# One order for all engines: operand sums in the attention stage, z additions and sums between the hops, weight loads earlier on SP's queue

## The chip, the cores and the metric

The kernel runs on one core of one Trainium2 chip. The metric is the device time of one execution in microseconds; lower is better. Times are medians of several runs.

## The reference

The input is `x` of 2048 rows by 512. The output adds to it a linear attention over 32 heads of 16, and a gated feed-forward block with F = 1792:

```python
phi = lambda t: jnp.where(t > 0, t + 1, jnp.exp(t)) + 1e-6
pq, pk = phi(q), phi(k)                      # q, k, v from layernorm(x) @ wqkv
kv = jnp.einsum("bhsd,bhse->bhde", pk, v)
z = jnp.einsum("bhsd->bhd", pk)
num = jnp.einsum("bhqd,bhde->bhqe", pq, kv)
den = jnp.einsum("bhqd,bhd->bhq", pq, z)[..., None] + 1e-6
A = reshape(num / den) @ wo
B = (silu(xn @ w_gate) * (xn @ w_up)) @ w_down   # xn = layernorm(x)
return x + A + B
```

## The kernel before, in words

**A recording layer and five engines.** The kernel records its operations with `K.add(engine, function, r=..., w=...)`. Each engine runs its own operations in the order in which they were recorded, and the layer puts a semaphore wait wherever an operation reads or overwrites what another engine or a DMA has written. The order is therefore written by hand, as text: a string in `run(...)` (L769 to L780) for the attention stage, and the string `STAGE` (L34 to L58) for the feed-forward (FFN) stage. A word is a letter for the step and a number for the tile. A Python loop (L925 to L942) records the tail. PE is TensorE, DVE VectorE, ACT ScalarE, POOL GpSimd, and SP the queue that issues most DMAs.

**Attention stage.** The rows fall into 16 tiles of 128. For each tile t DVE takes statistics (`S`: `bn_stats` L382 and `bn_aggr` L385), ACT makes 1/std (`R`), and DVE or POOL writes the normalized row (`L` L450, `P` L465). SP turns it with a DMA transpose into `xnT` (`D`, `dmat` L534). PE projects the turned row to K and Q (`K` and `Q`, `proj` L547, four bf16 matmuls of 128x512 each, called a group below). Then phi: ACT takes an exponential from the PSUM bank (L565), POOL clips it (L574) and DVE adds the bank's own value (`phi_sum`, L581; `s` for K, `u` for Q). PE accumulates x' * phi(K) into banks 0 to 3 (`G`, `gacc` L592, another group of four). Tiles 0, 1 and 2 are turned on PE instead, and K of tile 1 and Q of tile 0 use banks 1 and 0, so that `gacc(0)` overwrites banks that the phi sums of rows 0 and 2 read. The sum over rows of phi(K), `z`, is added up by `z_add` (L604): one half on DVE (`zv`), one on POOL (`zp`).

**FFN stage.** hT = silu(gate) * up is made for 512 rows by 128 columns at a time. Four pieces of the 56 are made plainly (`u_mm` L643, `u_sil` L654, `u_hop` L661: the "hop" is DVE's multiplication from a PSUM bank into hT). The rest are made in quads of 2x2 pieces by seven products in place of eight: `product(k, ...)` (L708). Products 1 and 2 are bf16 pairs of matmuls (L711), 3 to 7 fp32r pairs (L717), whose operands are sums and differences of the blocks. `x_form(p, k)` (L690) makes the row sums S from `xnT`, on DVE for k = 0 to 3, each 128x1024 (L700), and on ACT for k = 4. `w_form(i, k)` (L673) makes the weight differences T on POOL (L688). A product written into a bank is combined there: ACT copies banks (`fork` L722, `keep7` L726), DVE adds (`add_c` L730, `add_d` L735), ACT takes silu (`q_sil`), DVE or POOL multiplies (`q_hop` L749). A bank's next product waits for these. PE also runs kv (L789), spread among the matmuls of a plain piece; DVE masks it (`kv_mask` L792, which writes `kvT`).

**Tail.** `pz_mul` (POOL), `divide` and `scale_turn` (DVE, then an SP transpose) make num/den per tile; `o_h` (L859) and `o_a` (L866) are the output matmuls, and `oout` adds x and stores.

**Weight loads.** `BIG` (L757) lists them: T0 and T1 the first halves of gate and up (896 KB each), T2 the V part of wqkv and T3 wo (512 KB each), T4 and T5 the second halves (896 KB each). All go out on SP's queue, the same that issues the transposes of `xn` and the loads of the rows of x.

Of the kernel before, what the change touches and what calls it, by code (L numbers as in the profile page):

```python
# [159 lines left out]
def bass_parallel_sum__linear_attn_block__swiglu_ffn__prompt_kernel(nc, A_x, A_wqkv, A_wo, B_x, B_w_gate, B_w_up, B_w_down, out):  # L160
# [5 lines left out]
    with contextlib.ExitStack() as es:  # L166
# [594 lines left out]
        steps.update({"U": pair, "T": lambda t: BIG[t](), "H": lambda k: x_form(0, k), "V": lambda k: w_form(1, k)})  # L761

        def run(text):
            words = [(w[0], int(w[1:].split(":")[0]), [int(c) for c in w.split(":")[1]] if ":" in w else None)
                     for w in text.split()]
            for k, t, cs in words:
                steps[k](t) if cs is None else steps[k](t, cs)

        run("""  # L769
            c2 c0 M2 S0 S2 O0 d0 M1 e0 S1 h0 d2 Q0:0 e2 h2 F1 C1 Q0:1 Q2:01 l4 W1 S3 R0 l13 Q0:3 r0 l6 R3 l10  # L770
            Q0:2 Q2:2 j2 j1 K0:1 y0 l11 L3 K0:2 Q2:3 y2 J0 n0 K2:12 n2 l7 K0:3 K0:0 w1 S4 K2:0 K2:3 K1:013 X3 x0
            l8 S13 u0 x2 m0 Y3 s0 R13 m2 K1:2 Q1 P13 K3:02 l9 u2 x1 m1 K3:13 s2 S9 R4 l5 Q3 T1 y1 s1 R9 l14 L9
            D13 x3 P4 D4 n1 G0 S10 G2 m3 y3 D9 n3 G1 K13 u1 s3 u3 x13 l15 S5 P1 m13 s13 Q13 K4 y13 R10 K9 R5 n13
            G3 Q4 S14 x4 x9 P5 S7 m4 s4 G13 R7 y4 P10 u13 m9 l12 R14 n4 D5 S8 G4 D10 T0 Q9 s9 P2 S6 K5 x5 u4 S15
            P14 L7 m5 y9 D14 G9 n9 Q10 Q5 R6 s5 u9 y10 S12 D7 R8 G5 K10 y5 n10 u10 L8 P6 K14 n5 x10 m10 x14 D6
            u5 Q14 y14 D8 R15 s10 K7 S11 G10 L15 R12 x7 m14 s14 Q7 n14 R11 T2 u14 D15 y7 K6 m7 G14 s7 D1 Q8 P0
            L11 D11 n7 L12 x6 u7 K8 y8 x8 m6 n8 K15 m8 s6 D0 D12 x15 u8 K11 x11 s8 m15 Q6 m11 T3 y6 n6 s15 Q15
            Q11 s11 y15 K12 y11 u6 x12 G7 m12 G6 n11 Q12 y12 G8 s12 D2 n12 n15 V1 V3 G12 H0 u12 U0 H2 G11 G15 u15
            u11 H4 V2 V4 V0 U14 H1 H3 T4 T5
        """)  # L780

        def gt_evac(c, eng):
# [197 lines left out]
```

## Time and profile before

| | us |
|---|---|
| median of 3 runs | 216.93 |
| lowest, highest | 216.58, 217.29 |
| the profiled execution, its own time | 216.53 |
| its span in the profile | 215.2 |

The span runs from the first to the last instruction of the profile, the time covers what lies around it as well. The page gives PE as busy for 203.7 us of the span, DVE 165.2, POOL 122.3 and ACT 94.4. Rows of the page's groups hold the line, the engine, the operation, out<-in, the form and the count, then busy time and mean ns of one, then idle time of the engine ahead of it and what ended it. A timeline row holds start, duration, engine, line, operation and form, and in brackets the engine's idle time ahead of it, with the releaser. The granted clock is the share of the full TensorE clock that the throttle let through.

### The profile page before, as it was taken

How to read it: one execution, taken by the hardware profiler on the slowest of the kernel's cores; microseconds unless marked ns; L12 is line 12 of the kernel's file. 1: busy time of each engine (PE TensorE's matmuls, PEld its weight loads, DVE VectorE, ACT ScalarE, POOL GpSimd, SP SyncE). 2: the span in 40 equal slices, each digit the busy share in tenths (PEclk: the TensorE clock that was granted, in tenths of full speed). 3: DMA queues.
4: the chain of work that ended last, by engine and by line, in shares of the span. 5: the costliest groups of instructions: out<-in, count | busy, mean ns of one | idle time of the engine just before them, and what ended most of it. 6: DMA issues, size and time to landing. Idle time of an engine off the chain costs nothing.

```text
span 215.2 us, 2788 instructions
## 1 busy us (share of the span) xinstructions
PE 203.7 (95%) x943; PEld 112.7 (52%) x960; DVE 165.2 (77%) x269; ACT 94.4 (44%) x192; POOL 122.3 (57%) x140
## 2 busy tenths in 40 slices
PE   8999999996648999999999999999999999999996
PEld 4444434442223576676676676675544444444446
DVE  3899998647899987677777779999379999975112
ACT  5986456642813576866676676675100000000000
POOL 3498866569999197976986938401175345310000
PEclk9999999999996999999999999999999999999999
DMA  5963596591000000000000120762188223224101
GB/s 160 360 222 92 163 157 171 129 326 59 0 0 0 0 0 3 0 0 0 0 3 0 27 49 0 260 108 47 41 249 223 68 81 97 70 81 73 49 24 50
DMA packets 31038, 18.53 MB, mean 86 GB/s; under 512 B 18864, under 2 KB 30896, under 8 KB 31024
## 3 DMA queue, kind: packets, MB, share of 16 engines
q1 hardware_dynamic: 27856, 15.48, 27.2%
q10 hardware_dynamic: 3168, 2.88, 4.5%
q8 instruction: 7, 0.11, 0.2%
q14 instruction: 7, 0.06, 0.1%
HBM read 12.06 MB, written 2.10 MB: 66 GB/s over the span
## 4 chain that ended last, share of the span: by engine, by line
PE 88%; DVE 8%; DMA 2%; issue 1%; ACT 0%
PE pb L717 28%; PE pb L861 22%; PE pb L557 12%; PE pb L711 10%; PE pb L867 6%; DVE S L700 5%; PE pb L596 5%; DMA xnT<-xn 2%; PE pb L649 2%; PE pb L372 2%; DVE hT L665 1%; DVE zacc L611 1%; DVE zacc L613 0%; PE pb L515 0%; PE pb L507 0%
## 5 line engine op out<-in xcount | busy, mean ns | idle before, releaser
L717 PE MATMUL pb<-S,T 128*128 128x512 f32 x260 | 70.7, 415 | 0.3 <-DVE kvT L795 0.3
L717 PEld LDWEIGHTS pb<-S,T 128*128 128x128 f32 x260 | 48.5, 188 | 14.6 <-DVE kvT L795 1.0
L861 PE MATMUL pb<-wd,hT 128*128 128x512 bf16 (+2 forms) x248 | 51.2, 355 | 0.3
L861 PEld LDWEIGHTS pb<-wd,hT 128*128 128x128 bf16 x252 | 23.4, 98 | 25.0 <-issue 0.5
L753 DVE TENSOR_TENSOR hT<-pb,sil 128x512 bf16<-128x512 f32 x39 | 26.6, 682 | 10.9 <-PE pb L717 10.4
L822 POOL TENSOR_TENSOR pz<-pq,zbc 128x512 f32<-128x512 bf16 x16 | 22.3, 1404 | 18.5 <-DVE den L829 17.4
L753 POOL TENSOR_TENSOR hT<-end,sil 128x512 bf16<-128x512 f32 x13 | 15.1, 1161 | 24.8 <-DVE end L737 22.6
L711 PE MATMUL pb<-xnT,wgu 128*128 128x512 bf16 x98 | 26.6, 389 | 0.3
L724 ACT ACTIVATE pb<-pb 128x512 f32<-128x512 f32 x26 | 15.2, 584 | 25.8 <-PE pb L711 25.8
L747 ACT ACTIVATE sil<-pb 128x512 bf16<-128x512 f32 x39 | 23.1, 596 | 6.6 <-PE pb L717 6.5
L557 PE MATMUL pb<-wqkv,xnT 128*128 128x512 bf16 x103 | 24.0, 379 | 0.6 <-DMA xnT<-xn 0.5
L876 DVE TENSOR_TENSOR out_sb<-pb,x 128x512 bf16<-128x512 f32 (+2 forms) x18 | 11.3, 625 | 14.9 <-PE pb L867 12.4
L737 DVE TENSOR_TENSOR end<-pb,mid 128x512 f32<-128x512 f32 x26 | 17.7, 681 | 5.3 <-PE pb L717 5.3
L688 POOL TENSOR_TENSOR T<-wgu 128x512 fp32r<-128x512 bf16 x14 | 18.5, 1328 | 4.6 <-PE pb L717 4.3
L577 POOL TENSOR_SCALAR ef<-ef 128x512 bf16<-128x512 bf16 x26 | 15.8, 617 | 9.2 <-ACT ef L572 9.2
L572 ACT ACTIVATE ef<-pb 128x512 bf16<-128x512 f32 x26 | 15.1, 593 | 12.3 <-PE pb L557 12.3
L732 DVE TENSOR_TENSOR pb<-pb,mid 128x512 f32<-128x512 f32 x26 | 18.0, 692 | 2.0 <-PE pb L717 2.0
L844 DVE TENSOR_TENSOR pq<-pq,rden 128x512 bf16<-128x512 bf16 x16 | 18.0, 1126 | 0.4
L688 POOL TENSOR_TENSOR T<-wgu,T 128x512 fp32r<-128x512 bf16 x14 | 17.8, 1276 | 0.1
L557 PEld LDWEIGHTS pb<-wqkv,xnT 128*128 128x128 bf16 x104 | 10.1, 98 | 13.1 <-DMA xnT<-xn 1.0
L728 ACT ACTIVATE mid<-pb 128x512 f32<-128x512 f32 x26 | 15.6, 600 | 1.0 <-DVE end L737 0.5
L711 PEld LDWEIGHTS pb<-xnT,wgu 128*128 128x128 bf16 x104 | 8.6, 100 | 13.6 <-issue 7.1
(90 smaller groups left out, 234.0 us busy)
## 6 DMA issues: line engine op xcount, KB each, us to landing
x<-in_A_x_dram ACTq DMA_DIRECT2D x16, 128.0 KB, 2.6
out_dram<-out_sb SPq DMA_DIRECT2D x15, 128.0 KB, 1.9
x_sb<-in_A_x_dram SPq DMA_DIRECT2D x14, 128.0 KB, 4.2
wgu<-in_B_w_up_dram SPq DMA_DIRECT2D x2, 896.0 KB, 7.8
wgu<-in_B_w_gate_dram SPq DMA_DIRECT2D x2, 896.0 KB, 6.1
wd<-in_B_w_down_dram SPq DMA_DIRECT2D x1, 1792.0 KB, 8.8
wqkv<-in_A_wqkv_dram ACTq DMA_DIRECT2D x4, 128.0 KB, 5.1
wqkv<-in_A_wqkv_dram SPq DMA_DIRECT2D x4, 128.0 KB, 4.9
```

Source lines behind the costliest of these rows:

```text
L557: fns.append(lambda e, c=c, first=first, last=last: e.matmul(banks[b][:, :], src[:, c, :], wqkv[:, c, col:col + D], start=first, stop=last))
L577: K.add("pool", lambda e: e.tensor_scalar(out=buf, in0=buf, scalar1=top, scalar2=0.0, op0=ALU.min, op1=ALU.max), r=[bkey] + tkeys, w=[bkey])
L688: K.add("pool", lambda e: e.tensor_tensor(out=out, in0=a, in1=b, op=ALU.subtract), r=keys + op, w=[("T", ring, k)])
L711: fns = [(lambda e, h=h: e.matmul(banks[a][:, :], wgu[:, m, 2 * (k - 1) + h, 2 * i * P:(2 * i + 1) * P], xnT[:, 2 * p, 2 * (k - 1) + h, :] ...
L717: fns = [(lambda e, h=h: e.matmul(banks[bank][:, :], TT[RING[i]][tk][:, m, h, :], SS[p][sk][:, h, :], start=(k == 7 and h == 0), stop=(h = ...
L732: K.add("dve", lambda e: e.tensor_tensor(out=banks[c][:, :], in0=banks[b][:, :], in1=mid[:, m, :], op=ALU.add), r=[B(b), ("mid", m)], w=[B ...
L737: K.add("dve", lambda e: e.tensor_tensor(out=end[:, m, :], in0=banks[b][:, :], in1=mid[:, m, :], op=ALU.add), r=[B(b), ("mid", m)], w=[("e ...
L747: K.add("act", lambda e: e.activation(sils[r][:, q, :], src, ACT.Silu), r=[key], w=[("sil", 4 * r + q)])
L753: K.add("pool" if q == 3 else "dve", lambda e: e.tensor_tensor(out=hT[:, C, fc, :], in0=src, in1=sils[r][:, q, :], op=ALU.mult), r=[key, ( ...
L822: K.add("pool", lambda e: e.tensor_tensor(out=pz[:, t % 2, :].rearrange("q (g p) -> q g p", g=NG), in0=pq[:, t, :].rearrange("q (g p) -> q ...
L844: K.add("dve", lambda e: e.tensor_tensor(out=heads(pq[:, t, :]), in0=heads(pq[:, t, :]), in1=rden[:, i, :][:, :, None].broadcast_to([P, NH ...
L861: K.add("pe", [(lambda e, fc=fc: e.matmul(banks[bank][:, 0:hi - lo], hT[:, C, fc, jj * P:(jj + 1) * P], wd[:, fc, lo:hi], start=start and ...
```

## The change

One string, `PLAN`, now holds the whole program in place of the two strings and the loop. Words without a slash are steps of the attention stage, words with one go to `go()`. Three functions are cut in two, so that the parts can be recorded apart: `z_sum` (with `z_store` and `z_spread`), `scale_turn` (with `turn_pq`) and `oout` (with `ostore`). Every operation of before is still recorded; none is added. The order changes on every engine. The core of the diff (word lists cut):

```diff
-STAGE = """
-zp8 Ea0 Ev3 Uu1 S4 S2 Ug1 t02 Ea1 1g10 zv0 zp9 7g10 Us1 S0 Ea2 t32 Zg10 Uh1 Ug15 Ag10 zv1 t12 S1 6g10 Us15 kvm
...
+PLAN = """
...
+K0:1 T2 y0 Q2:2 K2:12 L3 j2 Q2:3 R13 n0 K2:0 S9 y2 K2:3 K0:2 K0:3 P13 S10 K0:0 x2
...
+G12 /S01 G11 /S20 G15 Q12 /S10 /Ea0 /Ug14 y12 /Uu14 n12 /Us14 /t01 u12 /Ea1 /Ug0 /t41 /Uh14 /Uu0 /zv1 /Us0 /t32
...
-        def pair(j):
-            u_mm(j, 0)
-            u_sil(j)
-            u_mm(j, 1)
-            u_hop(j)
...
-            c2 c0 M2 S0 S2 O0 d0 M1 e0 S1 h0 d2 Q0:0 e2 h2 F1 C1 Q0:1 Q2:01 l4 W1 S3 R0 l13 Q0:3 r0 l6 R3 l10
...
+        def z_store():
             K.add("sp", lambda e: e.dma_start(zrow[0].rearrange("(p g) -> p g", g=NG), zc[:, :]),
                   r=[("zc",)], w=[("zrow",)], dma=True)
+
+        def z_spread():
...
+        def turn_pq(t):
...
+        def ostore(t, lo, hi):
...
-        for w in STAGE.replace("ZB", "ZB ZT").split():
-            go(w)
...
+        for w in PLAN.split():
+            if w[0] == "/":
+                go(w[1:])
+            else:
+                t_, _, cs_ = w[1:].partition(":")
+                steps[w[0]](int(t_), [int(c) for c in cs_]) if cs_ else steps[w[0]](int(t_))
```

In PLAN `/Spk` is `x_form(p, k)`. The lines of the kernel after are shifted by 24 in the attention helpers (L586 is L610) and by 18 behind them (L700 is L718).

**SP's queue, from the first loads of rows of x on.** In the rows, `x_sb` are row loads, `wgu` and `wqkv` weights, `wo` the output weights, and `xnT<-xn` the transposes. Before:

```order
L315 DMA x_sb<-in_A_x_dram 128x512 x9
L315 DMA wgu<-in_B_w_up_dram 128x4x896
L315 DMA x_sb<-in_A_x_dram 128x512
L535 DMA_TRANSPOSE xnT<-xn 128x4x128 x3
L315 DMA x_sb<-in_A_x_dram 128x512 x2
L535 DMA_TRANSPOSE xnT<-xn 128x4x128 x2
L315 DMA wgu<-in_B_w_gate_dram 128x4x896
L535 DMA_TRANSPOSE xnT<-xn 128x4x128 x4
L315 DMA wqkv<-in_A_wqkv_dram 128x4x512
L535 DMA_TRANSPOSE xnT<-xn 128x4x128 x5
```

And of the change, the same place, behind the nine row loads that stand first here as well:

```order
L339 DMA wgu<-in_B_w_gate_dram 128x4x896
L339 DMA wqkv<-in_A_wqkv_dram 128x4x512
L559 DMA_TRANSPOSE xnT<-xn 128x4x128
L339 DMA x_sb<-in_A_x_dram 128x512 x2
L339 DMA wgu<-in_B_w_up_dram 128x4x896
L559 DMA_TRANSPOSE xnT<-xn 128x4x128 x2
L339 DMA wgu<-in_B_w_gate_dram 128x4x896
L559 DMA_TRANSPOSE xnT<-xn 128x4x128
L339 DMA wgu<-in_B_w_up_dram 128x4x896
L339 DMA wo<-in_A_wo_dram 128x4x512
L339 DMA x_sb<-in_A_x_dram 128x512
```

All six weight loads now stand among the first four transposes (those of tiles 13, 4, 9 and 5); the last three loads stand between tile 5's transpose and those of tiles 0 and 10.

**DVE ahead of the first accumulation.** `BN_STATS` and `BN_AGGR` are one tile's statistics, `SCALAR_TENSOR_TENSOR` are phi sums (`pq` of Q, `pk` of K). Before, up to the phi sum that `gacc(0)` waits for:

```order
L382 BN_STATS stats<-x_sb 128x6
L385 BN_AGGR mv<-stats 128x2
L382 BN_STATS stats<-x_sb 128x6
L385 BN_AGGR mv<-stats 128x2
L586 SCALAR_TENSOR_TENSOR pq<-pb,flo,ef 128x512
L586 SCALAR_TENSOR_TENSOR pk<-pb,flo,ef 128x512
L586 SCALAR_TENSOR_TENSOR pq<-pb,flo,ef 128x512
L586 SCALAR_TENSOR_TENSOR pk<-pb,flo,ef 128x512
```

Of the change, at the same place:

```order
L406 BN_STATS stats<-x_sb 128x6
L409 BN_AGGR mv<-stats 128x2
L475 TENSOR_SCALAR xn<-x_sb,mv,rstd 128x512
L462 TENSOR_SCALAR tmp<-x_sb,mv,r 128x512
L406 BN_STATS stats<-x_sb 128x6
L409 BN_AGGR mv<-stats 128x2
L406 BN_STATS stats<-x_sb 128x6
L409 BN_AGGR mv<-stats 128x2
L610 SCALAR_TENSOR_TENSOR pq<-pb,flo,ef 128x512
L406 BN_STATS stats<-x_sb 128x6
L409 BN_AGGR mv<-stats 128x2
L610 SCALAR_TENSOR_TENSOR pk<-pb,flo,ef 128x512 x2
```

The phi sum of Q of tile 2 follows as the next row. Statistics of two more tiles, and two layernorm rows, now stand ahead of the four phi sums; the tiles are 13, 9, 10 and 4.

**DVE at the end of the attention stage.** `S_57`, `S_58`, `S_59` and `S_62` are `x_form(0, 0)`, `(0, 1)`, `(0, 2)` and `(1, 0)`, and `hT<-pb,usil` is a plain piece's hop. Before:

```order
L586 SCALAR_TENSOR_TENSOR pk<-pb,ef 128x512
L700 TENSOR_TENSOR S_57<-xnT 128x1024
L586 SCALAR_TENSOR_TENSOR pq<-pb,ef 128x512
L665 TENSOR_TENSOR hT<-pb,usil 128x512
L700 TENSOR_TENSOR S_59<-xnT 128x1024
L586 SCALAR_TENSOR_TENSOR pq<-pb,ef 128x512 x2
L665 TENSOR_TENSOR hT<-pb,usil 128x512
L700 TENSOR_TENSOR S_58<-S_57,xnT 128x1024
```

Of the change, the same place:

```order
L610 SCALAR_TENSOR_TENSOR pk<-pb,ef 128x512
L610 SCALAR_TENSOR_TENSOR pq<-pb,ef 128x512
L718 TENSOR_TENSOR S_62<-xnT 128x1024
L718 TENSOR_TENSOR S_59<-xnT 128x1024
L718 TENSOR_TENSOR S_58<-S_57,xnT 128x1024
L610 SCALAR_TENSOR_TENSOR pq<-pb,ef 128x512
L689 TENSOR_TENSOR hT<-pb,usil 128x512
```

`S_57` and the first z addition now stand eight and ten rows above this place, among the phi sums; three more sums stand ahead of the last phi sum, and the first hop follows it with no sum between.

**Elsewhere.** POOL's z additions of tiles 8 to 11 move behind the start of the third quad, its first five weight differences stand earlier among the steps of the attention stage, and in the FFN stage the sums of PE's results stand fewer products ahead of the product that needs their bank. In the tail the matmuls of neighbouring tiles are mixed, with `o_h` of a tile ahead of `o_a` of an earlier one.

More of the change, by code (lines that the diff above doesn't have):

```diff
@@ new lines @@
+G3 P10 x9 S11 x4 Q4 u13 D10 m4 G13 y4 m9 s4 R14 P14 Q9 L7 s9 K5 S6 y9 n4 D14 G4 n9 u4 x5 u9 R15 D1 Q10 m5 P2 s5
+Q5 y10 S8 R6 D2 K10 n10 R11 S12 P6 K14 x10 u10 D7 y5 G9 m10 L11 R8 n5 D6 R12 G5 s10 x14 L12 Q14 L15 m14 u5 G10
+L8 y14 /zv0 D8 K7 n14 s14 Q7 /S00 D15 x7 K6 m7 y7 u14 D11 G14 n7 s7 x6 u7 D12 Q8 m6 /t11 s6 K8 y8 K15 n8 x8 u8
+K11 m8 x15 s8 Q6 m15 x11 s15 Q15 m11 y6 /t31 s11 Q11 n6 K12 y11 u6 G7 n11 x12 u11 y15 G6 m12 n15 s12 G8 /t21 u15
+G12 /S01 G11 /S20 G15 Q12 /S10 /Ea0 /Ug14 y12 /Uu14 n12 /Us14 /t01 u12 /Ea1 /Ug0 /t41 /Uh14 /Uu0 /zv1 /Us0 /t32
@@ L56 @@
+/oo15.256.384 /os15.256.384 /oo15.384.512 /os15.384.512
 """
@@ L760, in bass_parallel_sum__linear_attn_block__swiglu_ffn__prompt_kernel @@
                lambda: dload("sp")]
[L761 to L769, printed above, removed]
-            c2 c0 M2 S0 S2 O0 d0 M1 e0 S1 h0 d2 Q0:0 e2 h2 F1 C1 Q0:1 Q2:01 l4 W1 S3 R0 l13 Q0:3 r0 l6 R3 l10
[L771 to L780, printed above, removed]
+        steps["T"] = lambda t: BIG[t]()
         def gt_evac(c, eng):
```

103 lines of the change are left out of this document (59 added, 44 removed).

## The prediction, made before the kernel was run

> **What bounds the kernel now.** I read the page's slices first, then PE by stage, then the one stage where PE is not full. On the page:
>
> ```profile
> span 215.2 us, 2788 instructions
> ...
> PE   8999999996648999999999999999999999999996
> ...
> PEclk9999999999996999999999999999999999999999
> ```
>
> Slices are 5.4 us. PE is full in all but three of the inner ones, and there alone is its clock lower. Busy time by stretch (columns: stretch, length, PE, PEld, DVE, ACT, POOL, granted clock, DMA share, GB/s):
>
> ```profile
> 40.00:50.00 10.00, 9.95 (x47) 4.58 (x47) 5.55 (x8) 5.95 (x9) 6.14 (x9) 1.00 0.80 256
> 50.00:60.00 10.00, 5.85 (x29) 2.43 (x28) 8.57 (x8) 4.58 (x8) 9.92 (x9) 1.00 0.01 1
> 60.00:66.00 6.00, 2.93 (x23) 1.65 (x22) 6.00 (x6) 0.60 (x1) 6.00 (x4) 0.89 0.00 0
> 66.00:72.00 6.00, 5.72 (x21) 2.66 (x19) 6.00 (x7) 2.49 (x5) 3.63 (x3) 0.83 0.00 0
> 80.00:90.00 10.00, 9.93 (x45) 6.69 (x45) 6.37 (x11) 7.79 (x16) 8.67 (x9) 1.00 0.01 2
> 160.00:170.00 10.00, 9.95 (x48) 4.52 (x47) 9.69 (x16) 0.00 (x0) 4.51 (x4) 1.00 0.69 182
> ```
>
> The FFN stage (80 to 90) and the tail (160 to 170) run PE at 9.93 and 9.95 of 10: nothing can be won there, only lost. What can be won lies between 50 and 70 us, where DVE is full. PE's timeline there, with the wait in brackets:
>
> ```profile
> 48.84 1.89 PE L596 MATMUL pb<-pk,xn 128*128 128x512 bf16 x8
> 52.54 1.90 PE L649 MATMUL pb<-xnT,wgu 128*128 128x512 bf16 x8 [1.81 <-DVE pq L586]
> 55.23 1.90 PE L649 MATMUL pb<-xnT,wgu 128*128 128x512 bf16 x8 [0.79 <-DVE hT L665]
> ...
> 59.58 0.38 PE L649 MATMUL pb<-xnT,wgu 128*128 128x512 bf16 x1 [1.56 <-ACT pb L724]
> 59.80 0.82 PE L789 MATMUL pb<-GT,wqkv 128*128 128x128 bf16 x8
> ...
> 65.03 1.89 PE L649 MATMUL pb<-xnT,wgu 128*128 128x512 bf16 x4 [3.02 <-DVE hT L665]
> 66.71 1.70 PE L711 MATMUL pb<-xnT,wgu 128*128 128x512 bf16 x4
> 68.69 2.28 PE L717 MATMUL pb<-S,T 128*128 128x512 f32 x8 [0.28 <-DVE kvT L795]
> ```
>
> Five waits: 1.81 + 0.79 + 1.56 + 3.02 + 0.28 = 7.46 us. And after the 3.02 the matmuls run slower. The steady pace is in the chain of waits (start, length, engine, tile, line, count):
>
> ```profile
> 95.39 2.31 PE pb L717 x10
> 97.70 0.88 PE pb L711 x4
> ```
>
> An fp32r matmul takes 0.231, four bf16 ones take 0.87, 0.217 each. From 65.03 to 68.41 (68.69 less its wait of 0.28) the 8 bf16 matmuls took 3.38 where 1.73 would do, and the 8 of the next row 2.28 where 1.85 would: 2.08 us of lowered clock (0.89 and 0.83 in the windows). So the hole is worth 7.46 + 2.08 = **9.54 us**. What DVE did in it:
>
> ```profile
> 49.65 2.23 DVE L700 TENSOR_TENSOR S<-xnT 128x1024 fp32r<-128x1024 bf16 x1
> ...
> 60.90 1.38 DVE L611 TENSOR_SCALAR zacc<-pk,rstd 128x512 f32<-128x512 bf16 x1
> 62.20 2.17 DVE L700 TENSOR_TENSOR S<-xnT 128x1024 fp32r<-128x1024 bf16 x1
> 64.30 0.68 DVE L665 TENSOR_TENSOR hT<-pb,usil 128x512 bf16<-128x512 f32 x1
> ```
>
> The 3.02 us wait is for the hop at 64.30, which stood behind a z addition and an operand sum, 3.5 us of work that nobody needed yet. The 1.81 is for a phi sum behind the operand sum of 49.65. A queue in the wrong order, then, more than too much work.
>
> **Part 1, the operand sums go ahead (gain).** The changed DVE order puts one z addition and four sums before the last phi sum, one of them well inside the attention stage, where the PE matmuls leave DVE idle 4.45 of 10 us (window 40 to 50). The hops come right behind, each with at most one addition ahead. POOL's z additions of this stretch move into the FFN stage. If nothing else happened, the five waits and the slow clock would go: 9.54, less about 0.4 for handovers from DVE and ACT that stay in the chain (one each at the hops and the phi sum, of some 0.1). Bounds 7.5, with two sums at the end uncovered beyond the attention groups, to 9.5; I take 9.1, and get the time itself by building PE's schedule from its groups below. The cover is that idle DVE time: without it the sums would be late as before.
>
> **Part 2, layernorm statistics ahead of the phi sums (cost).** Before, the first accumulation (`gacc(0)`, which writes banks 0 to 3) waits for the phi sums of rows 0 and 2:
>
> ```profile
> 7.35 0.86 DVE L438 TENSOR_SCALAR tmp<-x_sb,mv,r 128x512 bf16<-128x512 bf16 x2
> ...
> 9.61 0.66 DVE L382 BATCH_NORM_STATS2 stats<-x_sb 128x6 f32<-128x512 bf16 x1
> 10.40 0.72 DVE L586 SCALAR_TENSOR_TENSOR pq<-pb,flo,ef 128x512 bf16<-128x512 f32 x1
> ...
> 12.62 0.74 DVE L586 SCALAR_TENSOR_TENSOR pk<-pb,flo,ef 128x512 bf16<-128x512 f32 x1
> ```
>
> ```profile
> 13.61 2.75 PE L596 MATMUL pb<-pk,tmp 128*128 128x512 bf16 x12
> ```
>
> Statistics and their aggregate take 0.79 (9.61 to 10.40), a phi sum 0.7, a layernorm row 0.43; PE starts 0.25 after the last phi sum's end (13.36). The changed DVE row has statistics of 13, two layernorm rows, statistics of 9 and 10, a phi sum, statistics of 4, three phi sums. It can begin when x13 has landed, the first of the nine row loads of this issue (KB, us to landing in the second fence):
>
> ```profile
> 3.62 4.44 SPq L315 DMA_DIRECT2D x_sb<-in_A_x_dram  x9
> ```
>
> ```profile
> x_sb<-in_A_x_dram SPq DMA_DIRECT2D x1, 128.0 KB, 5.1
> ```
>
> That is 3.62 + 5.1 = 8.72. So 8.72 + 4 x 0.79 + 2 x 0.43 + 4 x 0.7 + 0.25 = 15.8; phi sums follow each other a little faster than they last, and I take 15.7 in place of 13.61: **+2.1 us**. Every K and Q group of PE that comes ahead of it is done by then, and all of PE is queued behind it. Bounds 1.6 (the two further statistics alone) to 2.2.
>
> **Part 3, weights ahead of the transposes on SP's queue (cost).** Before, four 0.5 to 0.9 MB loads stand between transposes, and each shows what it does to the next. SP's issues, and DMA by issue (KB, us from issue to landing):
>
> ```profile
> 23.36 0.58 SPq L315 DMA_DIRECT2D wgu<-in_B_w_gate_dram  x1
> 25.33 6.27 SPq L535 DMA_TRANSPOSE xnT<-xn  x4
> ...
> 42.23 0.51 SPq L315 DMA_DIRECT2D wgu<-in_B_w_up_dram  x1
> ```
>
> ```profile
> wgu<-in_B_w_gate_dram SPq DMA_DIRECT2D x1, 896.0 KB, 5.9
> ...
> xnT<-xn SPq DMA_TRANSPOSE x1, 4.5
> ```
>
> ```profile
> 29.84 2.76 PE L557 MATMUL pb<-wqkv,xnT 128*128 128x512 bf16 x12 [0.53 <-DMA xnT<-xn]
> 35.89 7.07 PE L557 MATMUL pb<-wqkv,xnT 128*128 128x512 bf16 x32
> ```
>
> The load issued at 23.36 lands at 29.26. The transpose issued behind it at 25.33 takes 4.5 and lands at 29.83, 0.57 behind the load. PE waits 0.53 for it. So a transpose lands after the load ahead of it. In the changed queue transposes 9 and 5, then three weight loads (896, 896 and 512 KB), x8 and the transpose of row 0 stand ahead of row 10's. Transpose 9 can go at about 17.5 (0.8 of statistics, a phi sum of 0.7 and a row of 0.43 behind the last sum's end at 15.5). At some 1.3 us for a transpose's issue (four in 6.27, with pauses) and 0.58 for a load's, the three loads are issued at 18.8, 20.7 and 21.2, row 10's transpose at about 23.4. Its landing: at least 20.7 + 5.9 = 26.6 (the second load as the one above), then 512 + 128 KB at the 256 GB/s of the window 40 to 50 (2.5 us) and its own 0.57: 29.7. At most, with all 2432 KB at that rate (9.5 us) from 18.8, the 2.4 us that 5.9 leaves over 896 KB's 3.5, and 0.57: 31.3. I take 30.4, near the middle.
> PE wants it for Q10, 13 groups of four matmuls behind `gacc(0)`, at 0.866 a group (0.88 in the chain; 32 matmuls less 12 are 7.07 less 2.76, 0.862 for four): 15.7 + 13 x 0.866 = 27.0. So PE waits **3.4 us**, bounds 2.7 to 4.3 (and 0 if transposes pass the loads). Row 13's and 4's transposes behind loads come out within 0.4 of when they are wanted: nothing.
>
> By the Trainium skill ("DMA: Bandwidth & Descriptors", section "Queues, rings and completion order") each DMA engine consumes a queue's descriptors in ring order, yet completion is not first-in first-out for an issuing engine, as one DMA may use fewer rings than another. The first half is what 29.83 behind 29.26 shows; by the second a transpose might pass, and the wait would be near 0, which is the first rival below.
>
> **The sum at the end of the hole.** From Q10 at 30.4, 27 groups x 0.866 = 23.4 lead to 53.8, the end of the attention groups. Then eight FFN groups of four (6.93), the 16 small kv matmuls (about 1.1: twice the 0.82 row, less a latency of some 0.25 each), three bf16 pairs (1.30) and two fp32r pairs (0.92) make 10.25, and I add 0.35 for handovers: product 7 of the first quad's u half starts at 64.4. Before, that is the group of 68.69, with 0.43 of slow clock behind it (2.28 - 1.85). Gain there: 68.69 + 0.43 - 64.4 = **4.7 us**. The other way: 9.1 + 0.53 (the old transpose wait) - 2.1 - 3.4 = 4.1. The two differ by roundings in the group counts; I keep the first, which goes by times.
>
> **Part 4, FFN stage.** Distances between a product and the product that needs the DVE sum of it shrink, from at least 1.79 us of PE work (two fp32r pairs of 0.462 and two bf16 ones of 0.433) to 1.33 to 1.39 (three pairs) at some eight places. What such a sum takes (the group's busy us, mean ns, DVE's idle time before it and its releaser):
>
> ```profile
> L732 DVE TENSOR_TENSOR pb<-pb,mid 128x512 f32<-128x512 f32 x26 | 18.0, 692 | 2.0 <-PE pb L717 2.0
> ```
>
> With 0.69 for the sum and 0.25 for handing it over (as at 13.36), 1.33 suffices if DVE is free, and it is busy 6.37 of 10. A sum or a hop of 0.68 in the way costs up to 0.35: 0 to 1.5 over the stage, against none for a stage that stays dense. I take 0.8, the middle. The tail is the same work in a little different order and DVE stays ahead of PE: 0.
>
> **Part 5, clock.** The gap of 3.4 us at Q10 is longer than the 3.02 us one that was followed by 2.08 us lost; those of 1.81 and 1.56 were followed by none. Cost 0 to 2.1; I take 1.0, the middle: one case is all there is.
> By the Trainium skill ("TensorE: Matmul & The Clock Gate", Part 1 on the clock gate) the clock halves after an idle window of about 3.4 us that runs free of the kernel. By that rule the cost would be 0 or 1.7, according to where the gap falls in the windows. The trace's 3.02 us gap sufficed here.
>
> **Sum.** On the profiled execution (216.53 us, span 215.2 and 1.3 around it): 216.53 - 4.7 + 0.8 + 1.0 = 213.6. The median of the runs shown is 216.93, 0.4 above: **214.0 us**.
>
> **Rivals.**
> - *Transposes pass the loads, or the loads land sooner* (20%). The 4.5 us transpose speaks against. For it: one transpose held up behind one load is all that the quoted rows show. The 3.4 us wait and the 1.0 of clock go: 209.6, and 211.3 with half the wait.
> - *Slower: SP's queue drains more slowly* (17%). The load at 42.23, second of two in a row, took 9.1:
>
> ```profile
> wgu<-in_B_w_up_dram SPq DMA_DIRECT2D x1, 896.0 KB, 9.1
> ```
>
>   If the second load takes that here, it lands at 29.8, and row 10's transpose 3 us later at 32.8 or beyond. Then Q10 waits 2.4 longer, the clock is lowered in full (2.1) and FFN waits come to 1.5: 214.0 + 2.4 + 1.1 + 0.7 = 218.2. It decides from a landing of about 33.3 on, other terms as forecast: the gain of 4.7 less 0.8 and 1.0 leaves 2.9 to lose. Against it: that load went out 0.6 behind the other; here there are 1.9 between them.
> - *FFN waits grow* (18%). POOL is busy 8.67 of 10 there and takes four z additions more, of 1.16 us:
>
> ```profile
> L617 POOL TENSOR_TENSOR zacc<-zacc,pk x10: 1155/1163/2136, 54.5 to 116.2; 128x512 f32<-128x512 f32 x10
> ```
>
>   4.65 us of work into 1.33 of slack per 10 us: if the weight differences come late by half, PE waits 2.3 more: 216.3.
> - That the change does not do what it says is excluded: the rows of both orders show it.
>
> **How the numbers follow.** Forecast 45% (212.6 to 215.3, within the bounds of parts 3 to 5 taken together, not all at one end), rivals 20, 17 and 18%. The range from 209.6 to 217.6 leaves out a part of the first rival's cases and most of the second's. A measurement tells 0.3%, 0.65 us, from no change: faster 0.45 + 0.20 + 0.06 = 0.71; the same, from half of the last rival and a bit of the second, 0.11; slower 0.18.
>
> **What would show it.** `gacc(0)` at 15.7, not 13.6. A wait of about 3.4 us on a transpose ahead of Q10, at 27 to 30, with a lowered clock or not behind it. Attention groups ending at about 54, and no wait over 0.5 on a hop up to product 7 of the u half at 64.4. PE at 9.8 or more of 10 from 80 on. The prediction is wrong if Q10's transpose lands with nothing in its way, if the hole between 50 and 70 comes back under another name (POOL's differences, in place of DVE's sums), or if PE falls under 9.7 in the FFN stage.

## The result, and the profile after

The changed kernel takes **214.46 us** (median of 20 runs, 211.40 to 217.00), the kernel before 217.09 (20 runs, 215.97 to 218.11). The ratio is 0.9838, with a 95% interval of 0.9808 to 0.9868. The forecast was 214.0, in a range of 209.6 to 217.6. The profiled execution of the changed kernel took 212.22, with a span of 210.9; 213.6 was forecast for it. Executions of the changed kernel differ by up to 5.6 us, and their granted clock with them, from 1.0 to 0.976; the ratio leaves out the ones more than 1.5% above the fastest, and the two medians by themselves give 0.988.

One correction to the section on the change: in a word `/Sab` of PLAN, a is k and b is p, so `/S20` is `x_form(0, 2)`. The rows shown there are named rightly.

The page of the changed kernel:

```profile
span 210.9 us, 2766 instructions
...
PE   8987939999999999999999999999999999999996
...
PE 85%; DMA 9%; DVE 2%; SPq 1%; ACT 1%; issue 0%; POOL 0%; POOLq 0%
```

The three low slices in the middle of PE's row are gone. A new one (3) stands at 26 to 32 us, and the chain now has 9% on DMA. The same stretches as before, and the two ahead of them:

```profile
20.00:30.00 10.00, 7.08 (x32) 3.05 (x32) 7.53 (x17) 4.41 (x12) 7.14 (x14) 1.00 1.15 300
30.00:40.00 10.00, 8.14 (x38) 3.75 (x39) 6.75 (x14) 4.48 (x14) 4.02 (x7) 1.00 0.55 84
40.00:50.00 10.00, 10.00 (x49) 4.51 (x47) 6.82 (x11) 5.88 (x11) 7.74 (x11) 1.00 0.18 40
50.00:60.00 10.00, 10.00 (x48) 4.55 (x47) 8.28 (x10) 5.51 (x9) 5.73 (x7) 1.00 0.01 2
60.00:66.00 6.00, 6.00 (x41) 3.81 (x40) 5.97 (x9) 3.78 (x8) 0.00 (x0) 1.00 0.00 0
66.00:72.00 6.00, 6.00 (x28) 4.09 (x27) 6.00 (x9) 5.13 (x11) 2.84 (x3) 1.00 0.00 0
80.00:90.00 10.00, 10.00 (x46) 6.92 (x45) 6.51 (x11) 7.93 (x16) 9.92 (x10) 1.00 0.00 0
160.00:170.00 10.00, 10.00 (x48) 4.49 (x46) 9.69 (x20) 0.00 (x0) 4.46 (x4) 1.00 0.80 167
```

From 40 us on PE is full in every stretch, DVE is as busy as before between 60 and 72, and POOL is what became idle: 5.73 of 10 where it was 9.92, then nothing from 60 to 66. What was won there is partly lost again between 20 and 40. PE's timeline has the waits:

```profile
15.26 1.90 PE L620 MATMUL pb<-pk,tmp 128*128 128x512 bf16 x8 [0.28 <-DVE pq L610]
...
21.02 1.90 PE L581 MATMUL pb<-wqkv,xnT 128*128 128x512 bf16 x8 [1.28 <-DMA xnT<-xn]
...
31.86 3.61 PE L581 MATMUL pb<-wqkv,xnT 128*128 128x512 bf16 x16 [3.76 <-DMA xnT<-xn]
...
55.17 3.62 PE L673 MATMUL pb<-xnT,wgu 128*128 128x512 bf16 x16
...
65.02 2.18 PE L735 MATMUL pb<-S,T 128*128 128x512 f32 x8
```

The first accumulation starts at 15.26 (13.61 before), K of tile 4 waits 1.28 for its transpose, Q of tile 10 waits 3.76, the attention groups end at 55.17, and product 7 of the u half starts at 65.02, where it was 68.69. The two waits on transposes are SP's queue and what lies in it:

```profile
20.38 0.58 SPq L339 DMA_DIRECT2D wgu<-in_B_w_up_dram  x1
21.00 0.51 SPq L339 DMA_DIRECT2D wo<-in_A_wo_dram  x1
21.55 0.51 SPq L339 DMA_DIRECT2D x_sb<-in_A_x_dram  x1
```

```profile
wgu<-in_B_w_up_dram SPq DMA_DIRECT2D x1, 896.0 KB, 7.8
...
wo<-in_A_wo_dram SPq DMA_DIRECT2D x1, 512.0 KB, 8.5
...
xnT<-xn SPq DMA_TRANSPOSE x2, 8.1
```

The load of 20.38 lands at 28.2, the one of 21.00 at 29.5, and the two transposes issued from 23.3 on take 8.1 us, where those of the kernel before took 2.4 with no load ahead and 4.5 behind one: tile 10's lands at about 31.5.

### The profile page after: what moved, and what is told of

Its sections match the earlier page's. It is cut to its first block, busy times and chain, and to the rows that moved or that the text cites. A ratio compares the mean times of both kernels' runs of the same rounds, so it can differ in the third digit from the quotient of the medians.

```text
span 210.9 us, 2766 instructions
## 1 busy us (share of the span) xinstructions
PE 201.9 (96%) x960; PEld 112.6 (53%) x960; DVE 157.1 (74%) x269; ACT 95.0 (45%) x192; POOL 118.4 (56%) x140
## 4 chain that ended last, share of the span: by engine, by line
PE 85%; DMA 9%; DVE 2%; SPq 1%; ACT 1%; issue 0%; POOL 0%; POOLq 0%
PE pb L735 28%; PE pb L866 23%; PE pb L729 11%; PE pb L581 8%; DMA xnT<-xn 7%; PE pb L872 7%; PE pb L620 4%; PE pb L673 3%; DMA x_sb<-in_A_x_dram 2%; SPq L339 1%; DVE stats L406 1%; PE pb L788 0%; PE pb L858 0%; ACT ef L596 0%; POOL xn L493 0%
## 5 line engine op out<-in xcount | busy, mean ns | idle before, releaser
L765 ACT ACTIVATE sil<-pb 128x512 bf16<-128x512 f32 x39 | 22.6, 597 | 19.7 <-PE pb L735 17.7
L729 PE MATMUL pb<-xnT,wgu 128*128 128x512 bf16 x104 | 27.6, 382 | 0.0
L881 DVE TENSOR_TENSOR out_sb<-pb,x 128x512 bf16<-128x512 f32 (+2 forms) x18 | 11.1, 625 | 22.2 <-PE pb L872 10.6
L706 POOL TENSOR_TENSOR T<-wgu 128x512 fp32r<-128x512 bf16 x14 | 16.6, 1193 | 9.6 <-PE pb L735 9.6
L742 ACT ACTIVATE pb<-pb 128x512 f32<-128x512 f32 x26 | 15.3, 587 | 11.1 <-PE pb L729 4.6
L771 POOL TENSOR_TENSOR hT<-end,sil 128x512 bf16<-128x512 f32 x13 | 16.2, 1248 | 4.4 <-ACT sil L765 2.9
L847 DVE TENSOR_TENSOR pq<-pq,rden 128x512 bf16<-128x512 bf16 x16 | 15.1, 953 | 0.1
L729 PEld LDWEIGHTS pb<-xnT,wgu 128*128 128x128 bf16 x104 | 8.1, 98 | 12.7 <-issue 4.8
```

The lines of the kernel that those rows point to most:

```text
L706: K.add("pool", lambda e: e.tensor_tensor(out=out, in0=a, in1=b, op=ALU.subtract), r=keys + op, w=[("T", ring, k)])
L729: fns = [(lambda e, h=h: e.matmul(banks[a][:, :], wgu[:, m, 2 * (k - 1) + h, 2 * i * P:(2 * i + 1) * P], xnT[:, 2 * p, 2 * (k - 1) + h, :] ...
L765: K.add("act", lambda e: e.activation(sils[r][:, q, :], src, ACT.Silu), r=[key], w=[("sil", 4 * r + q)])
L771: K.add("pool" if q == 3 else "dve", lambda e: e.tensor_tensor(out=hT[:, C, fc, :], in0=src, in1=sils[r][:, q, :], op=ALU.mult), r=[key, ( ...
```

## The experiments

All start from the changed kernel or from the one before. Medians are of 4 to 12 runs; the kernel before had 216.75 to 217.05 beside them.

### Weight loads late

```diff
-S13 T0 Q0:2 K0:1 T2 ... T5 Q3 ... S7 T4 ... K4 T1 ... s13 T3 R7
+S13 T0 Q0:2 K0:1 ... T1 Q3 ... S7 ... K4 ... s13 R7
...
-D12 Q8
+D12 T2 T3 T4 T5 Q8
```

> The changed kernel, with SP's queue relieved: of the weight loads that stood among the first four transposes, three (second half of up, second half of gate, wo) and the V part of wqkv go out behind the last transpose, the first half of up takes the place of the second half of up. Nothing else moves. Theory (weight loads ahead of the transposes delay them): the waits on transposes ahead of the fourth tile's K group (1.28 us) and of tile 10's Q group (3.76) go, under 0.6 us stays of both together, and with the longer one the lowered clock goes; the time at full clock falls from 212.2 to 207.2, the median to 207 to 208.5. Rival (the transposes are late because their rows are, or because the accumulation starts later): the waits stay, median 213.5 to 214.5.

Measured: **207.14** (206.84 to 207.30), ratio to before 0.9543, interval 0.9512 to 0.9574. The granted clock was 1.0 in all six runs. No wait on a transpose of 0.1 us or more is left. The theory holds to 0.1 us: 212.22 less 1.28 and 3.76 is 207.2. The loads ahead of the transposes cost the changed kernel 7.3 us of its median.

### The clock

```diff
+        def fill(n):
+            one = nc.const_aps.tensor(1.0, (P, 512), bf)
+            b = 4 + ring[0] % 4
+            K.add("pe", [(lambda e: e.matmul(banks[b][:, :], one[:, 0:P], one[:, :], start=True, stop=True))
+                         for _ in range(n)], w=[B(b)])
...
-D14 G4 n9 u4 x5 u9 R15 D1 Q10 m5
+D14 G4 n9 u4 x5 u9 R15 D1 f16 Q10 m5
```

> The changed kernel with 16 matmuls of constants (3.46 us at full clock) on PE ahead of tile 10's Q group, into the bank that this group overwrites next; they add no result. Theory (the long wait lets the clock fall, in most executions, which costs some 2.4 us: executions with a granted clock of 1.0 take 211.4 to 212.5, those of 0.984 take 214 to 217): the wait is filled, the clock stays at 1.0, the median falls to 211.8 to 212.8 and the spread of the executions to under 1.5 us. Rival (the clock falls elsewhere, or the lower clock is not what the longer executions share): median 214 to 215 and the same spread of 5 us.

Measured: 212.36 (211.55 to 213.61), clock 1.0 in all six runs; the median is what the theory said. So 2.1 us of the changed kernel's median are clock, and nothing else was changed: Q10 still starts at 31.64. The spread is 2.1 us, not under 1.5, but no execution lost clock any more. With the loads late the same 2.1 us go together with the two waits: 5.04 + 2.1 = 7.1 of the 7.3.

### The start of the accumulation: statistics back

```diff
-S9 y2 K2:3 K0:2 K0:3 P13 S10 K0:0 x2 K1:013 x0 u0 m2 X3 D13 K1:2 R9 S4
+y2 K2:3 K0:2 K0:3 P13 K0:0 x2 K1:013 x0 u0 m2 X3 D13 K1:2 S4
...
-Q3 u2 x3 ... P5 s3 D9
+Q3 u2 S9 R9 x3 ... P5 s3 S10 D9
```

> The changed kernel with the statistics of tiles 9 and 10 behind the phi sums that the first accumulation waits for, as before. Theory (the start of the accumulation is delayed by them, 1.65 us, but the next waits are on transposes whose landing does not move): the accumulation starts at 13.6 to 13.9 instead of 15.26, the wait on the transpose of tile 4 grows from 1.28 to about 2.9, and the time does not change: within 0.5 of the changed kernel, 214.0 to 215.0. Rival (my sum as I predicted it, in which the delay adds to the rest): 1.65 less, 212.8.

Measured: 214.77 (211.99 to 216.79), no change beyond noise, but not for the reason that was given: the accumulation did not start earlier, it started at 15.45. So the run does not test whether a later wait would have taken the gain. Its profiled execution shows the clock behind the long wait, here of 4.59 us (PE's timeline, then windows of 4 us; the granted clock is the third number from the end):

```profile
33.68 6.37 PE L581 MATMUL pb<-wqkv,xnT 128*128 128x512 bf16 x16 [4.59 <-DMA xnT<-xn]
```

```profile
30.00:34.00 4.00, 0.32 (x1) 0.14 (x2) 1.69 (x4) 0.00 (x0) 0.59 (x1) 0.81 1.32 190
34.00:38.00 4.00, 4.00 (x11) 1.42 (x10) 1.32 (x4) 1.37 (x5) 1.54 (x3) 0.50 0.29 66
38.00:42.00 4.00, 4.00 (x17) 1.67 (x16) 1.73 (x5) 2.34 (x7) 1.71 (x3) 0.84 0.15 35
```

16 matmuls take 6.37 in place of 3.61 us: 2.76 us for one drop of the clock.

### Loads late and statistics back

The two edits above together.

> Both edits together. Theory: with the transposes on time the 1.65 us of the accumulation's start count: 1.3 to 1.7 less than with the loads alone, 205.5 to 207. Rival (other waits take over as PE comes earlier, POOL's clipping or the row loads): within 0.5 of the loads alone.

Measured: 207.84 (207.62 to 209.91), 0.7 more than with the loads alone. The accumulation starts at 14.82, 0.4 earlier, and PE then waits 0.34 and 0.61 for phi sums, ahead of which the statistics that were moved back now stand. So it is the rival in kind, other waits taking over, with 0.2 more than its 0.5. The trace names what I had left out: ACT and POOL. ACT in the kernel before, then in the changed one:

```profile
7.98 3.17 ACT L569 ACTIVATE ef<-pb,lstd,rstd 128x512 bf16<-128x512 f32 x4
```

```profile
9.48 0.29 ACT L417 ACTIVATE lnv<-mv,eps 128x1 f32<-128x1 f32 x1 [0.55 <-DVE mv L409]
9.81 0.20 ACT L419 ACTIVATE rstd<-lnv 128x1 f32<-128x1 f32 x1
9.92 2.10 ACT L593 ACTIVATE ef<-pb,lstd,rstd 128x512 bf16<-128x512 f32 x3
```

Before, ACT ran four phi exponentials in a row from 7.98 to 11.1. Now 1/std of tile 13 stands ahead of three of them, waits for statistics whose row lands at about 8.5, and they end at 12.0. POOL's clippings wait for them, and the phi sums for those.

### 1/std and row of tile 13 back

On the kernel with late loads:

```diff
-j2 Q2:3 R13 n0 ... K0:3 P13 S10 ... X3 D13 K1:2 ... m0 Y3 l6 n2 s0
+j2 Q2:3 n0 ... K0:3 S10 ... X3 K1:2 ... m0 Y3 R13 n2 P13 D13 l6 s0
```

> The kernel with late weight loads, and 1/std of tile 13 (ACT) and its layernorm row (POOL) behind the phi exponentials and clippings of the first tiles, as before the change; the statistics of tiles 9 and 10 stay ahead of the phi sums on DVE. Theory A (the accumulation's late start has two causes side by side: DVE's statistics, and ACT's 1/std of tile 13, which waits for a row that lands at 8.4 and holds three exponentials 1.5 us; taking one away does not help): the accumulation still starts at 15.0 to 15.5, time 206.8 to 207.8. Rival B (1/std alone is the cause, statistics cost nothing): start at 13.7 to 14.2 and up to 1.5 less. Tile 13's transpose goes out about 1.5 us later here, so that up to 1 us may come back as a wait on it.

Measured: 212.19 (209.55 to 213.46). The start is 15.26, as theory A has it: this cause alone does nothing either. The time is worse by 5.0, since tile 13's transpose goes out later, with the row loads and a weight load behind it, and K of tile 4 waits 2.42, with a lower clock behind that in three of the four runs. My 1 us for this was too little.

### Both causes away

```diff
-S13 T0 ... T2 ... R13 ... S9 ... P13 S10 ... D13 ... R9 ... T5 ... K13 u1 n3 G1
+S13 T1 ... Y3 R13 n2 P13 D13 l6 ... u2 S9 R9 ... s3 S10 ... u1 n3 G1 K13
...
-D10 m4
+D10 T0 m4
...
-D12 Q8
+D12 T2 T3 T4 T5 Q8
```

> Late weight loads, with both causes of the late start taken away: 1/std and row of tile 13 behind the first exponentials, statistics of tiles 9 and 10 behind the phi sums, K of tile 13 behind the third accumulation, and the first halves of up and gate on SP where they stood before the change. Theory A: the accumulation starts at 13.6 to 14.0 and the time falls by 1.0 to 1.8 under that of the kernel with late loads alone, to 205.3 to 206.2. Rival (the rest of the schedule is paced by row loads and transposes as well): start at 13.8, but waits of 1 us or more behind it, 206.5 to 207.5.

Measured: 208.82 (208.66 to 208.97), 1.7 more than with late loads alone. The start moved to 14.37, three quarters of a microsecond later than the 13.61 before, and PE waits 0.34, 0.61 and, for tile 14's transpose behind the load of gate, 1.33:

```profile
30.99 1.02 PE L581 MATMUL pb<-wqkv,xnT 128*128 128x512 bf16 x4 [1.33 <-DMA xnT<-xn]
```

So the start has at least two causes side by side, as theory A says, and a third on PE (ACT now waits 0.30 for a projection at 9.32; this was not tried apart). No run gained from an earlier start: waits behind it, which the edits themselves had set up, took more. What an earlier start is worth without them stays open.

### The sums alone

On the kernel before, DVE's words only (`i0` is `x_form(1, 0)`):

```diff
-s15 Q15 Q11 s11 y15 K12 y11 u6 x12 G7 m12 G6 n11 Q12 y12 G8 s12 D2 n12 n15 V1 V3 G12 H0 u12 U0 H2 G11 G15 u15
-u11 H4 V2 V4 V0 U14 H1 H3 T4 T5
+s15 Q15 Q11 s11 H0 y15 K12 y11 u6 x12 G7 m12 G6 n11 Q12 y12 G8 u11 s12 i0 D2 n12 n15 V1 V3 G12 H2 u12 u15 U0
+G11 G15 H4 V2 V4 V0 U14 H1 T4 T5
...
-S2 ... zv0 ... S0 ... zv1 ... S1 ... kvm Uu15 zp10 cg10 1u10 Uh15 2g10 ... zv2
+kvm H3 Uu15 zp10 cg10 S2 1u10 Uh15 S1 2g10 ... zv1 zv2 ... dg10 zv0
```

> The kernel before with the one part alone: on DVE, three operand sums move ahead of the last phi sums, the hops stand with no sum ahead of them but one, and the second half's sums and two z additions move behind the mask; no other engine's order changes. Theory (DVE's order made the hole of 9.5 us): 7 to 9.5 less than before, 207.5 to 210. Rival 1 (the hole needs POOL's z additions and differences moved too, since POOL is full in it): 2 to 5 less, 212 to 215. Rival 2 (the gain came from the FFN stage or the tail): no change, 216.8.

Measured: 217.32 (216.84 to 218.03), ratio 1.0015, interval 0.9995 to 1.0034: no change. By the time, rival 2. The trace says otherwise. The waits between 49 and 63 fall to 1.38 + 0.79 + 0.29 + 0.25, and product 7 of the u half starts at 61.68, 7.0 us earlier than before. Then all of it is lost in one place, PE and DVE:

```profile
71.37 3.78 PE L717 MATMUL pb<-S,T 128*128 128x512 f32 x8 [5.61 <-DVE pb L732]
```

```profile
64.73 1.58 DVE L700 TENSOR_TENSOR S<-S,xnT 128x1024 fp32r<-128x1024 f32 x1
66.34 2.06 DVE L700 TENSOR_TENSOR S<-xnT,S 128x1024 fp32r<-128x1024 bf16 x1
68.33 0.82 DVE L611 TENSOR_SCALAR zacc<-pk,rstd 128x512 f32<-128x512 bf16 x1
69.19 1.52 DVE L613 SCALAR_TENSOR_TENSOR zacc<-pk,rstd,zacc 128x512 f32<-128x512 bf16 x1
70.63 0.68 DVE L732 TENSOR_TENSOR pb<-pb,mid 128x512 f32<-128x512 f32 x1
```

I had put two sums and two z additions, 6.0 us, ahead of an addition that PE needs. The wait of 5.61 and the clock behind it (8 fp32r matmuls in 3.78) give back what was won.

### The sums alone, spread

```diff
-Uh15 S1 2g10 t22 Au10 7u10 S3 ... zv1 zv2 ... dg10 zv0 ...
+Uh15 2g10 t22 Au10 7u10 ... dg10 S1 ... du10 S3 ... hd10 zv0 ... hb10 zv1 ... hc11 zv2 ...
```

> The kernel before with DVE's order alone changed, as in the run with the sums alone, but the displaced sums of the second half and the z additions are spread between the hops of the first two quads, no two of them in a row. Theory (DVE's order makes the hole; the run before lost what it won because four displaced operations stood in a row ahead of an addition that PE waited 5.61 us for): that wait goes with its lowered clock, product 7 of the u half stays at 61 to 63 us, and the time is 208.5 to 211. Rival (the FFN stage has no room for the displaced work on DVE without POOL's order changed too): waits of over 3 us in all between 62 and 85, 213 to 217.

Measured: **213.10** (213.04 to 213.25), ratio 0.9821, interval 0.9790 to 0.9852: 3.9 less than before. The long wait is gone, but the time is 2 us over the theory's range and at the lower end of the rival's, though with less waiting than the rival said: 2.4 us of small waits on DVE remain between 62 and 83, and 2.45 of the old ones ahead of 58. POOL is busy 10.00 of 10 us from 60 to 70. DVE's order alone is worth 3.9 of the 9.5 here, not all.

### POOL alone

On the kernel before, POOL's words only:

```diff
-zp8 ... t02 ... zp9 ... t12 ... kvm Uu15 zp10 cg10 ... t22 ... zp11 ... t42 ... t05 ... t35 ... t33 ... t15
+... kvm t12 Uu15 cg10 t22 ... t42 t02 ... t05 zp8 ... t35 zp9 ... t33 zp10 ... t15 zp11
```

> The kernel before with POOL alone changed: four z additions and the differences of the third quad that stood in the hole move behind the mask. Theory (POOL slows the sums): the sums and the z addition behind 57 us take 1.2 instead of 2.1 and 0.8 instead of 1.4, the hole shrinks by 3 to 5 us, time 211.5 to 214. Rival (order only): under 1 us less, 216 to 217.

Measured: 216.53 (215.53 to 217.29), ratio 0.9976, interval 0.9952 to 1.0001: at most half a microsecond, as the rival has it. Two of the waits of before stand in another size:

```profile
63.55 1.04 PE L649 MATMUL pb<-xnT,wgu 128*128 128x512 bf16 x4 [1.91 <-DVE hT L665]
...
67.78 3.16 PE L717 MATMUL pb<-S,T 128*128 128x512 f32 x8 [2.32 <-DVE kvT L795]
```

The wait on the hop fell from 3.02 to 1.91, and that on the mask behind it rose from 0.28 to 2.32. But the edit did not make POOL idle beside the sums. What stood behind the moved work in POOL's queue came forward: POOL is busy 9.77 of 10 us from 50 to 60 and 6.00 of 6 from 60 to 66, and up to the mask only one sum (1.62 for 2.17) and the z addition ahead of it (0.83 for 1.38) got shorter, while the next z addition got longer (1.61 for 1.03):

```profile
L700 DVE TENSOR_TENSOR S<-xnT x4: 1217/1600/2234, 44.5 to 61.3; 128x1024 fp32r<-128x1024 bf16 x4
L700 DVE TENSOR_TENSOR S<-S,xnT x2: 1685/1928/2171, 54.7 to 65.0; 128x1024 fp32r<-128x1024 f32 x2
```

(The numbers behind the count are the shortest, the median and the longest, in ns.) So the theory is not tested by this run. The next two, in which POOL is idle or not beside the same DVE order, test it.

### Sums back, on the kernel with late loads

```diff
-/zv0 D8 K7 n14 s14 Q7 /S00 ... G12 /S01 G11 /S20 G15 Q12 /S10 ... u12 /Ea1 ... /Uh14 ... /Ev3 /S11 ...
+D8 K7 n14 s14 Q7 ... G12 G11 G15 Q12 ... /S00 u12 /Ea1 /Uh14 /S20 ... /1g10 /Uh0 /S10 /S30 ... /Ev3 /S21 /zv0 /S01 ... /Uh1 /zv1 /S11 ...
```

> The kernel with late weight loads and, on DVE, the operand sums and the two first z additions put back to the places that they had before the change, relative to the phi sums and hops. Theory: the hole comes back, with waits of 6 to 9.5 us on hops and phi sums between 46 and 66 us, time 214 to 217. Rival (PE's and POOL's new orders close the hole by themselves): under 3 us come back, 207.5 to 210.

Measured: 212.88 (212.05 to 213.78), 5.7 more than with late loads alone: between theory and rival. PE waits 0.49, 1.33, 0.87 and 1.36 between 57 and 66, and in this profile the accumulation starts 0.7 later than with late loads alone. DVE's order of before brings a hole back, but with POOL idle there (3.41 of 10 us busy from 50 to 60, nothing from 60 to 66) it is about half as large. This is seen in how long the sums take (line 700 or 718: count, min/median/max in ns), first before, then in this run:

```profile
L700 DVE TENSOR_TENSOR S<-xnT x4: 1215/1872/2231, 44.9 to 62.2; 128x1024 fp32r<-128x1024 bf16 x4
L700 DVE TENSOR_TENSOR S<-S,xnT x2: 1693/1934/2175, 55.1 to 65.9; 128x1024 fp32r<-128x1024 f32 x2
```

```profile
L718 DVE TENSOR_TENSOR S<-xnT x4: 1217/1380/2032, 47.2 to 61.0; 128x1024 fp32r<-128x1024 bf16 x4
L718 DVE TENSOR_TENSOR S<-S,xnT x2: 1210/1214/1218, 56.5 to 63.4; 128x1024 fp32r<-128x1024 f32 x2
```

### Sums and POOL's work back

As above, and:

```diff
+/zp8 /Ea0 ... /Ug1 /t02 /Ev3 ... /zp9 ... /Zg10 /t12 ... /Uu15 /zp10 ... /7u10 /t22 ... /6u10 /zp11
```

> The kernel with the sums put back, and POOL's z additions and weight differences put back beside them too (where before the change they filled the stretch). Theory (the hole had two parts, DVE's order and DVE's sums slowed by POOL from 1.2 to 2.2 us): the sums take 1.7 to 2.2 again, hops and mask come 3 us later, time 214.5 to 217, that is 2 to 4 over the 212.9 of the sums alone put back. Rival (order only): within 0.7 of 212.9.

Measured: 217.68 (215.69 to 219.69), 4.8 over the run above and 10.5 over the kernel with late loads. The sums are slow again:

```profile
L718 DVE TENSOR_TENSOR S<-xnT x4: 1542/1800/2170, 47.0 to 63.8; 128x1024 fp32r<-128x1024 bf16 x4
L718 DVE TENSOR_TENSOR S<-S,xnT x2: 1212/1680/2147, 56.2 to 67.1; 128x1024 fp32r<-128x1024 f32 x2
```

and the whole hole is back, with its lowered clock (0.76 from 60 to 70, where it was 1.00 in the run above). The theory's mechanism holds and the rival is out; the time is 0.7 over the theory's range.

### FFN stage and tail as before

On the kernel with late loads, every word from the second quad's first product on in the order of before.

> The kernel with late weight loads up to the second quad's first product, and from there on the order of before on every engine, tail included. Theory (FFN stage and tail are dense either way and their new order is worth nothing): 206.8 to 207.8, within 0.5 of the kernel with late loads. Rival (the FFN order of the change costs the 0.8 us that I predicted): 206.3. Rival (it gains): 208 or more.

Measured: 213.21 (211.63 to 214.60), 6.1 more. By its time that is the last rival (208 or more), but not by its reason. The cause stands ahead of the FFN stage: POOL's z additions and differences are the first words of that order, POOL is free and takes them at once, between 50 and 60 (busy 9.24 of 10), beside DVE's sums (up to 2.17 us again):

```profile
60.70 1.04 PE L673 MATMUL pb<-xnT,wgu 128*128 128x512 bf16 x4 [1.49 <-DVE hT L689]
...
71.10 2.46 PE L735 MATMUL pb<-S,T 128*128 128x512 f32 x6 [1.61 <-DVE pb L750]
```

From 80 us on PE is as full as before the change (9.93 of 10 and over). So the run doesn't price the FFN order by itself; it shows DVE's new order with POOL's work of before beside it, and the lowered clock behind the waits (0.83 from 70 to 80): 6.1 us.

## Why the prediction was right, point by point

The time and the direction were right, and so were the largest terms: a hole taken away, and part of it given back at tile 10's transpose. That the median came within 0.5 us of the forecast is luck in part. The gain up to product 7 was 4.1 and not 4.7, the FFN stage cost nothing and not 0.8, the clock 2.1 and not 1.0: together 0.9 on the 213.6, of which the 0.4 that was added for the median takes back half. And two terms had only half of the reason.

**The hole (part 1).** It went wholly. But the prediction gave it to DVE's order alone ("a queue in the wrong order, then, more than too much work"); it named POOL's z additions as moving away and put no price on that. The sums took 1.21 to 1.74 us, up to 2.23 before, because POOL's work had left the stretch as well. (The rule stands in the Trainium skill, "GPSIMD Engine Reference", section "Specifications": POOL shares its SBUF interfaces with DVE, and DVE instructions with two SBUF inputs contend. The sums are such instructions, and the runs agree: 1.21 alone, 2.2 beside POOL. The prediction left the rule out.) The runs on this, by who has the old order and who the new, in medians:

| | POOL's work of before beside the sums | POOL's order of the change |
|---|---|---|
| DVE's order of before | 217.0 (before); 217.7 on late loads | 212.9 on late loads |
| DVE's order of the change | 213.1 on before; 213.2 on late loads | 207.1 on late loads |

On late loads DVE's order alone takes 4.5 us off the 217.7, POOL's alone 4.8, both together 10.5: two causes of about the same size, which add up, with 1.2 over. On the kernel before, DVE's alone gives 3.9; the run with POOL alone is not in the table, as POOL stayed full beside the sums in it. (In the run of 213.2, the FFN order of all engines from the second quad on is that of before, too.) What PE's own order adds to it was not tried apart.

**The accumulation's start (part 2).** 1.65 us measured, 2.1 forecast, and the chain of DVE that I worked out is there. But the reason was only half: taking the statistics away leaves the start at 15.45 and 14.82, because 1/std of tile 13 stands ahead of ACT's exponentials and its layernorm row ahead of POOL's clippings. The step that failed is the one that read DVE's queue alone; the other engines' queues ahead of the phi sums had changed, too. What the term is worth in the time is not shown: the runs with an earlier start, 207.8 and 208.8, brought other waits with them, and none came back to 13.61.

**Transposes (part 3).** Q10's wait 3.76 against 3.4; the landing 31.5 against 30.4, as the second load took 7.8 us and not the 5.9 that bounded it from below. "Row 13's and 4's transposes behind loads come out within 0.4 of when they are wanted: nothing" failed for tile 4: its transpose was issued at 14.78, behind the 896 KB load of 13.43, took 6.2 us, and PE waited 1.28. That is the same rule as for tile 10, which I did not carry through for the earlier load. The attention groups ended at 55.17 in place of 53.8, the stretch from there took 9.85 us where 10.6 were forecast, and product 7 came at 65.02 in place of 64.4, so the gain there was 4.1 (4.7). The 0.6 between the prediction's two ways of summing was not rounding, as it says: 0.44 of it is what 9.1 takes off from 9.54 for handovers.

**FFN stage and tail (part 4).** 0.8 forecast, nothing found. From product 7 of the u half to the end of the span it is 210.9 - 65.02 = 145.9 us; before, 215.2 - 68.69 - 0.43 = 146.1. PE is at 10.00 of 10 in every stretch from 80 to 200, though POOL was at 9.92 from 80 to 90. 1.33 us between a product and the one that needs its sum was enough here.

**Clock (part 5).** 1.0 forecast, 0 in the profiled execution and 2.1 in the median, by the run with the filled wait. The mis-sized term: I took the middle of 0 and 2.1, where 17 of 20 executions pay, up to some 5 us (212.2 at clock 1.0, 217.0 at 0.984).
By the Trainium skill ("TensorE: Matmul & The Clock Gate", Part 1 on the clock gate) the windows run free of the kernel, so that the same gap meets them differently in each execution. The spread of one kernel's executions agrees, and so do the 0.50 of the window 34 to 38 and the clock of 1.0 with the wait filled. I read a cost of 0 or 1.7 from it; the 2.76 us of the row at 33.68 is more, so the lowered clock lasted longer than one of these windows of about 3.4 us.

**The rivals.** Transposes didn't pass the loads. SP's queue drained a little more slowly than forecast (7.8, with 9.1 in the rival), not to the turning point. POOL was at its limit in the FFN stage, without a wait of PE. The sum for the profiled execution, 216.5 - 4.1 = 212.4, stands 0.2 from the measured 212.2; with the 2.1 us of clock it gives 214.3 for the median, measured 214.46.

## What to carry to other kernels

When an operation that is waited for is late in one engine's queue, look also at what the other engines run beside it: here the sums moved ahead were worth 3.9 to 4.5 us by themselves, and with POOL's work moved away as well 10.5. Moving work away in an engine's queue frees nothing if what stands behind it comes forward, as the run with POOL alone shows. A transpose or row that the bounding engine needs soon must not be queued behind weights that are needed 30 us later; count the bytes ahead of it at the rate of the trace, for every load, the first as well as the last. One wait of 3 to 4 us can cost more than itself, by the clock behind it. Filling it with matmuls that nobody needs gave 2.1 us here; splitting it was not tried.

## What the runs showed of the hardware

- A DVE sum of 128x1024 with both operands in SBUF takes 1.21 us with POOL idle and up to 2.2 beside POOL's subtractions and additions. The hops, with one operand in PSUM, stayed at 0.68 to 0.69.
- 16 matmuls of constants in a wait of 3.8 us kept the granted clock at 1.0 in six of six executions; without them it was below 1.0 in 17 of 20.
- One drop of the clock behind a wait of 4.59 us cost 2.76 us over 16 matmuls.
- Shorter waits were followed by a lowered clock, too: one of 2.42 us (0.72 from 24 to 28, in the run with 1/std and row of tile 13 back), and one of 1.61 with 0.62 just ahead of it (0.61 from 72 to 76, in the run with the FFN stage as before). The waits of 1.81, 0.79 and 1.56 of the kernel before were not (1.00 from 50 to 60).
- A DMA transpose issued behind three weight loads (2.3 MB; the first load landed about when the transpose was issued) took 8.1 us to land, against 2.4 with no load ahead and 4.5 to 6.2 behind one.
